# Weight pieces written to SBUF in runs of 1024 or 768 columns instead of 512 or 384

## The chip, the cores and the metric

The kernel runs on one core of a Trainium2 chip. A core has a matrix engine (PE, with its weight loads shown apart as PEld), a vector engine (DVE), a scalar engine (ACT), a general engine (POOL) and a queue engine (SP), an on-chip memory of 128 partitions (SBUF) that they share, and an accumulator memory (PSUM) that PE writes. Sixteen DMA engines move data between the chip's main memory and SBUF. The metric is the device time of one execution in microseconds; before the change the median of three runs is 322.45 us (322.34 to 323.88).

## The reference

Attention for 8 batches, 12 heads, 448 positions and a head dimension of 64, with one extra term in the softmax's denominator, and then a soft mixture of 8 experts with 4 slots each over the 3584 resulting rows:

```python
scores = scale * np.matmul(q, k.transpose(0, 1, 3, 2))
m = np.max(scores, axis=-1, keepdims=True)
e = np.exp(scores - m)
attn = e / (np.sum(e, axis=-1, keepdims=True) + np.exp(-m) + 1e-09)
x = matmul(attn, v)                       # as rows: 3584 x 768
logits = x @ phi                          # 3584 x 32
d = softmax of logits over the rows       # dispatch
slot_input = d.T @ x                      # 32 x 768, 4 slots for each expert
h = np.maximum(slot_input[e] @ w1[e], 0)  # w1[e]: 768 x 1024
slot_out[e] = h @ w2[e]                   # w2[e]: 1024 x 768
c = softmax of logits over the slots      # combine
return c @ slot_out
```

All inputs are float32. The expert weights w1 and w2 are 8 x 768 x 1024 and 8 x 1024 x 768: 50 MB in main memory, 25 MB once they are bfloat16 in SBUF.

## The kernel before

The attention is cut into U = 24 units, each a pair of batches and a pair of heads, and each unit into TB = 7 steps. A step of the main loop (line 802) issues the score matmuls of one step (stage_S, line 256), the transposed scores and their exponentials ten steps behind (stage_ST, lines 300, 305, 309), and whatever the dictionary `plan` holds for that step: the transposes of q and k of the next unit (stage_T, line 241), the product with v (stage_AV, line 336), the normalised rows (stage_N, line 364, on POOL), the transposes of these rows (line 419) and the router's logits. So the order of the work on every engine is written out by hand; nothing is moved by a scheduler.

The expert weights are loaded in 32 pieces in the background of the attention and used only after it, in two passes: w1 in `experts_hidden` (matmul at line 709) and w2 in `outer` (line 825). Piece i is one half of one expert's matrix, 128 partitions of 3072 bfloat16 columns; pieces 0 to 15 are w1 (three rows of 1024 columns a partition), the others w2 (four rows of 768). Pieces 0 to 23 have a place of their own in the tile `wres`, 24 rooms of 3072 columns; pieces 24 to 31 go into `block` once the attention's buffers there are free. A piece of the first kind is loaded as two DMAs of 64 partitions each (lines 782 to 785), at steps 1 and 3 of each of the middle units, some at other places: 48 DMAs at line 180. The remaining 13 DMAs of line 180 are those into `block`, from about 251 us on.

The function `room(i, n)` gives the place of piece i. In `wres` two neighbouring pieces share two rooms and alternate in turns of n columns:

```python
pair = wres[:, ds(i // 2 * 2, 2), :].rearrange("p a n -> p (a n)")
return pair.rearrange("p (k a n) -> p k a n", a=2, n=n)[:, :, i % 2, :]
```

So a piece's columns lie in SBUF in runs of n, each followed by a run of the other piece. The load (load_w, line 167) asks for a room with n // 2, half a row of the weight matrix, 512 columns for w1 and 384 for w2, and views the source in the same halves. A DMA run is then 512 or 384 columns: 2048 or 1536 bytes of float32 read, 1024 or 768 bytes of bfloat16 written. In `block` a piece lies in one stretch. The users take the dictionary `W[kind, e, j]`, a row of the matrix as two halves, and index the half.

The DMAs that change their type on the way (q, k and the weights, float32 to bfloat16) are issued by POOL and go over queue q0; v, which stays float32, is issued by SP (line 159) over q1, and so are the stores of the result (line 889). In each unit POOL issues in this order: the first weight DMA, the normalising product of line 364, the cast of v to bfloat16 (line 314), the second weight DMA, then two q and two k DMAs (line 136) for two units on, which wait until PE has transposed the unit before out of the same buffer. The DMAs of a queue are taken in the order of their issue.

Of the kernel before, what the change touches and what calls it, by code (L numbers as in the profile page):

```python
# [24 lines left out]
def kernel(  # L25
# [93 lines left out]
    def room(i, n):  # L119

        if i >= WRES:
            return block[:, ds(rooms[i - WRES], HW)].rearrange("p (k n) -> p k n", n=n)

        pair = wres[:, ds(i // 2 * 2, 2), :].rearrange("p a n -> p (a n)")
        return pair.rearrange("p (k a n) -> p k a n", a=2, n=n)[:, :, i % 2, :]
# [35 lines left out]
    W = {}  # L161
# [5 lines left out]
    def load_w(i, j0=0, m=None, p0=0, rows=128):  # L167


        kind, e, half = weights[i]  # L170
        if kind == 1:
            J, n = KC // 2, F
            src = moe_w1[e].rearrange("(p j) f -> p j f", p=128)[:, ds(half * J, J), :]
        else:
            J, n = FK // 2, DD
            src = moe_w2[e, ds(half * 128 * J, 128 * J)].rearrange("(p j) f -> p j f", p=128)
        js = ds(2 * j0, 2 * (m or J))
        t_ = room(i, n // 2)
        src = src.rearrange("p j (h n) -> p (j h) n", h=2)
        gdma(out=t_[ds(p0, rows), js, :], in_=src[ds(p0, rows), js, :])  # L180
        for j in range(j0, j0 + (m or J)):
            W[kind, e, half * J + j] = t_[:, ds(2 * j, 2), :]

    first_loads()

# [246 lines left out]
    def mixture(bp, n, at):  # L432
# [98 lines left out]
        if final:  # L531
            at(n - 28, "end", lambda: logits((0, 1)))
            at(n - 2, "end", lambda: logits((2, 3, 4), close=False))
            at(n, "end", lambda: logits((5,)))
            at(n, "end", lambda: gate_logits(0))
            at(n, "end", lambda: warm(1))
            at(n + 2, "small", slot_max)
            at(n + 3, "small", slot_exp)
            at(n + 3, "small", lambda: last_state["lT"]())
            at(n + 4, "end", slots_T)  # L540
            at(n + 4, "end", lambda: last_state["gl"][0]())
            at(n + 4, "end", lambda: warm(1))
            at(n, "load", lambda: nc.gpsimd.memset(SI, 0.0))
            at(n + 5, "small", slot_sum)
            at(n + 7, "end", slot_in)
            at(n + 7, "end", lambda: [load_w(WRES + i) for i in (6, 7)])
            at(n + 7, "end", lambda: gate_logits(1))
            at(n + 7, "end", lambda: last_state["gl"][1]())
            at(n + 7, "end", experts_in)
            at(n + 7, "end", experts_hidden)  # L550
        else:
            for j in range(0, HP, 2):
                at(n - 7 * (HP - 2 - j), "end", lambda j=j: logits((j, j + 1)))
            at(n + 2, "end", slot_max)
            at(n + 5, "end", slot_exp)
            at(n + 6, "value", slots_T)
            at(n + 7, "small", slot_sum)
            at(n + 8, "value", slot_in)
# [195 lines left out]
    for u in range(U):  # L754
        n = u * TB
# [28 lines left out]
    for i, n in enumerate(halves):  # L784
        at(n, "load", lambda i=i: load_w(i // 2, 0, None, i % 2 * P, P))
# [5 lines left out]
    for n, i, js in ((end - 6, 0, (0, 2)), (end - 5, 0, (2, 2)), (end - 2, 1, ()), (end + 2, 2, ()),  # L791
                     (end + 4, 3, (0, 1)), (end + 7, 3, (1, 2)), (end + 9, 3, (3, 1)), (end + 9, 4, (0, 3)),
                     (end + 12, 4, (3, 1)), (end + 12, 5, (0, 3)), (end + 18, 5, (3, 1))):
        at(n, "load", lambda i=i, js=js: load_w(WRES + i, *js))
# [125 lines left out]
```

## Time and profile before

| | |
|---|---|
| median of three runs | 322.45 us |
| the profiled execution | 324.77 us, of which the span from first to last instruction is 323.0 us |
| PE busy | 278.7 us |
| POOL busy | 227.6 us |
| mean granted PE clock | 0.961 (1.00 up to about 290 us) |
| packets on all DMA queues | 48826, 59.34 MB |
| POOL issues of line 180 into wres | 48, 733 ns each on average |
| weight DMA into wres, issue to landing | median 5.7 us |
| q and k DMA into block, issue to landing | median 6.1 and 6.3 us |

The page of the profile gives each engine's busy time, the DMA queues with their packets, bytes written and the time that their packets took as a share of 16 engines, the chain of work that ended last, and the costliest groups of instructions. In a group a column tells how long the engine stood idle before these instructions and what ended it; "issue" there is time in which the engine waited for nothing that the profile shows. A table of stretches gives for each stretch its length, then for each engine its busy time and the number of instructions, the granted PE clock, the DMA share and the GB/s written. The trace also holds a record of every DMA packet: queue, size written, start and duration.

### The profile page before, as it was taken

To read this page: it belongs to the slowest core of one execution; us is meant where nothing else is said; L and a number is where in the kernel's file an instruction comes from. 1 tells how busy PE (TensorE), PEld (TensorE's weight loads), DVE (VectorE), ACT (ScalarE), POOL (GpSimd) and SP (SyncE) were. 2 spreads that over 40 slices of the span, in tenths; PEclk is the share of its full clock that TensorE was granted. 3 is DMA by queue.
4 is the path that set the end of the run, shared out by engine and by line. 5 is a ranking of instruction groups with operands and counts; after the bars stand their busy time and mean duration, and the time that the engine had idled before them with its cause. 6 is when DMAs were issued, how large, how long until landed. Compare 5 with 4: busy or idle time off the path is not lost.

```text
span 323.0 us, 13361 instructions
## 1 busy us (share of the span) xinstructions
PE 278.7 (86%) x5874; PEld 160.4 (50%) x5874; DVE 256.0 (79%) x342; ACT 212.4 (66%) x337; POOL 227.6 (70%) x334
## 2 busy tenths in 40 slices
PE   1669999979999999998999999999999886996910
PEld 1325555546546666555556566555555444652300
DVE  2988988978899999997899999988998845437720
ACT  3025868767778788785777888777877893237610
POOL 6476798888898888987898799989983854620000
PEclk9999999999999999999999999999999999999555
DMA  7979999999999999999899989999998899947997
GB/s 136 157 89 185 172 155 204 180 183 163 174 187 186 143 154 185 182 185 155 131 168 197 156 131 205 167 186 149 162 193 170 117 184 198 194 100 282 398 400 287
DMA packets 48826, 59.34 MB, mean 184 GB/s; under 512 B 4512, under 2 KB 44192, under 8 KB 48768
## 3 DMA queue, kind: packets, MB, share of 16 engines
q0 software_dynamic: 37568, 36.46, 75.8%
q1 hardware_dynamic: 11200, 22.02, 20.4%
q8 instruction: 46, 0.75, 0.9%
q14 instruction: 12, 0.10, 0.1%
HBM read 83.46 MB, written 11.01 MB: 292 GB/s over the span
## 4 chain that ended last, share of the span: by engine, by line
PE 70%; DVE 11%; issue 5%; DMA 4%; POOL 3%; ACT 2%; SPq 0%; DVEq 0%; ACTq 0%; POOLq 0%
PE av L336 16%; PE ps L256 12%; PE ps L300 11%; PE ps L305 8%; PE ps L241 6%; DVE block L264 4%; PE ps L884 3%; PE ps L419 3%; DMA block<-in_k_dram 3%; DVE m L264 2%; PE ps L260 2%; PE ps L825 2%; ACT block L309 2%; PE ps L709 2%; DMA wres<-in_q_dram 1%
## 5 line engine op out<-in xcount | busy, mean ns | idle before, releaser
L309 ACT ACTIVATE block<-ps 128x896 bf16<-128x896 f32 x168 | 153.9, 918 | 57.4 <-PE ps L305 54.4
L264 DVE TENSOR_REDUCE block<-ps 128x2 bf16<-128x896 f32 x84 | 90.8, 1090 | 13.2 <-PE ps L256 11.5
L264 DVE TENSOR_REDUCE m<-ps 128x2 bf16<-128x896 f32 x84 | 90.8, 1091 | 8.8 <-PE ps L256 7.4
L336 PE MATMUL av<-block 64*128 64x65 bf16 (+1 forms) x2688 | 90.4, 194 | 4.7 <-issue 4.0
L336 PEld LDWEIGHTS <-block 64*128 64x128 bf16 (+1 forms) x2688 | 75.6, 97 | 34.5 <-issue 12.6
L300 PE MATMUL ps<-block,ones 64*64 64x448 bf16 x672 | 70.0, 369 | 3.6 <-POOL block L288 1.3
L305 PE MATMUL ps<-block 64*64 64x448 bf16 x672 | 66.5, 354 | 2.0 <-issue 2.0
L256 PE MATMUL ps<-block 64*128 64x448 bf16 x288 | 54.1, 371 | 3.8 <-DVE m L264 1.3
L256 PEld LDWEIGHTS <-block 64*128 64x128 bf16 x288 | 19.8, 94 | 53.0 <-issue 48.4
L282 POOL TENSOR_TENSOR block<-mt,nmask 128x768 bf16<-128x768 bf16 x24 | 35.2, 1469 | 14.3 <-ACT mt L276 12.6
L136 POOL DMA_DIRECT2D block<-in_q_dram x46 | 27.5, 602 | 19.1 <-PE ps L241 17.6
L364 POOL TENSOR_TENSOR block<-block,rec 128x896 bf16<-128x896 f32 x21 | 35.8, 1706 | 0.5
L180 POOL DMA_DIRECT2D wres<-in_moe_w_dram x48 | 35.1, 733 | 1.4
L300 PEld LDWEIGHTS <-ones 64*64 64x64 bf16 x672 | 24.7, 106 | 8.4 <-issue 3.2
L136 POOL DMA_DIRECT2D block<-in_k_dram x46 | 27.8, 620 | 1.2 <-ACT block L309 1.2
L244 DVE COPY block<-ps 128x896 bf16<-128x896 bf16 x48 | 27.8, 617 | 0.3
L305 PEld LDWEIGHTS <-block 64*64 64x64 bf16 x672 | 24.5, 107 | 2.9 <-issue 2.7
L241 PE MATMUL ps<-ident,block 128*64 128x128 bf16 x644 | 24.5, 229 | 0.7 <-DVE m L264 0.4
L314 POOL CAST block<-block 128x896 bf16<-128x896 f32 x24 | 22.5, 938 | 0.8 <-PE ps L305 0.8
L241 PEld LDWEIGHTS <-block 128*64 128x64 bf16 x644 | 20.4, 115 | 3.8 <-issue 1.7
L347 ACT COPY block<-av 128x780 f32<-128x780 f32 x22 | 17.7, 806 | 1.0 <-PE av L336 0.6
L420 DVE COPY block<-ps 128x896 bf16<-128x896 bf16 (+1 forms) x23 | 14.0, 608 | 5.5 <-PE ps L419 5.3
(161 smaller groups left out, 254.5 us busy)
## 6 DMA issues: line engine op xcount, KB each, us to landing
wres<-in_moe_w_dram POOLq DMA_DIRECT2D x48, 384.0 KB, 5.7
out_dram<-wres SPq DMA_DIRECT2D x28, 384.0 KB, 4.6
block<-in_v_dram SPq DMA_DIRECT2D x46, 224.0 KB, 6.1
block<-in_q_dram POOLq DMA_DIRECT2D x46, 112.0 KB, 6.1
block<-in_k_dram POOLq DMA_DIRECT2D x46, 112.0 KB, 6.3
block<-in_moe_w_dram POOLq DMA_DIRECT2D x4, 768.0 KB, 8.4
block<-in_moe_w_dram POOLq DMA_DIRECT2D x3, 384.0 KB, 5.7
block<-in_moe_w_dram POOLq DMA_DIRECT2D x2, 576.0 KB, 8.0
```

The costliest lines, as they stand in the source:

```text
L136: eng.dma_start(out=t_[ds(b * P, P), :, :], in_=src[bp * 2 + b, ds(hp * 2, 2)].rearrange("h (p t) d -> p h (t d)", t=TB))
L180: gdma(out=t_[ds(p0, rows), js, :], in_=src[ds(p0, rows), js, :])
L241: nc.tensor.transpose(ps[ds(h * D, D), :, ds(t * P, P)], r[:, h, ds(t * D, D)], ident)
L244: nc.vector.tensor_copy(t_, ps)
L256: nc.tensor.matmul(ps[:, h, ds(0, S)], QT[u][hs, b, ds(c * 128, 128)], KT[u][hs, b, :], start=True, stop=True)
L264: nc.vector.tensor_reduce(m[:, :, s], ps[:, :, ds(0, S)], axis=AX.X, op=ALU.max)
L282: nc.gpsimd.tensor_tensor(md[:, :, ds(0, C3 * 128)].rearrange("p b (e n) -> p b e n", n=P), mt.unsqueeze(1).unsqueeze(1).broadcast_to([128 ...
L300: nc.tensor.matmul(ps[ds(b * P, P), h, ds(0, S)], ones[hs, :], MD[u][hs, b, :], start=True, stop=False)
L305: nc.tensor.matmul(ps[ds(b * P, P), h, ds(0, S)], KT[u][hs, b, ds(t * P, P)], QT[u][hs, b, :], start=False, stop=True)
L309: nc.scalar.activation(et, ps[:, :, ds(0, S)], AF.Exp, scale=scale)
L336: nc.tensor.matmul(o, et[bs, h, ds(c * 128, w)], V65[u][bs, h, t, ds(0, 65)], start=(t == 0 and h == 0 and c == 0), stop=(t == TB - 1), sk ...
L364: (nc.gpsimd if u < U - 3 else nc.vector).tensor_tensor(x.rearrange("p s (h d) -> p h s d", h=2), xv[:, :, :, ds(0, D)], rec.unsqueeze(3). ...
```

## The change

The load asks for a room with turns of a whole row of the weight matrix, n = 1024 columns for w1 and 768 for w2, and no longer splits the source's rows. Two neighbouring pieces in `wres` still alternate, in turns twice as long. A DMA run is then 4096 or 3072 bytes read and 2048 or 1536 bytes written. `W` still hands out a row as two halves, so its users are as before, as are the order of all instructions, the number of DMAs, and the loads into `block`, whose runs are contiguous in either form.

```diff
         else:
             J, n = FK // 2, DD
             src = moe_w2[e, ds(half * 128 * J, 128 * J)].rearrange("(p j) f -> p j f", p=128)
-        js = ds(2 * j0, 2 * (m or J))
-        t_ = room(i, n // 2)
-        src = src.rearrange("p j (h n) -> p (j h) n", h=2)
+        js = ds(j0, m or J)
+        t_ = room(i, n)
         gdma(out=t_[ds(p0, rows), js, :], in_=src[ds(p0, rows), js, :])
         for j in range(j0, j0 + (m or J)):
-            W[kind, e, half * J + j] = t_[:, ds(2 * j, 2), :]
+            W[kind, e, half * J + j] = t_[:, j, :].rearrange("p (h n) -> p h n", h=2)
```

## The prediction

> **What bounds the kernel now.** I read the page's busy line and DMA queues first, then the waits of the matmul engine, then a table of stretches between its stalls, then the DMA queues inside two short windows.
>
> ```profile
> PE 278.7 (86%) x5874; PEld 160.4 (50%) x5874; DVE 256.0 (79%) x342; ACT 212.4 (66%) x337; POOL 227.6 (70%) x334
> DMA  7979999999999999999899989999998899947997
> ...
> q0 software_dynamic: 37568, 36.46, 75.8%
> q1 hardware_dynamic: 11200, 22.02, 20.4%
> q8 instruction: 46, 0.75, 0.9%
> ...
> L180 POOL DMA_DIRECT2D wres<-in_moe_w_dram x48 | 35.1, 733 | 1.4
> ```
>
> PE is the bound (the chain that ended last is 70% PE), and the DMA engines have a packet on record nearly all the time. q8 matters more than its 0.9%: 46 packets of 0.75 MB in all are 16 KB each, and 0.75 MB over PE's 5874 + 5874 instructions is 64 bytes for each, so q8 carries PE's own program, 256 instructions (128 matmuls with their weight loads) to a packet.
>
> ```profile
> PE av L336 <- issue: 4.0, 8, 0.8
> PE ps L305 <- issue: 2.0, 2, 1.4
> PE ps L419 <- issue: 1.7, 1, 1.7
> ...
> PE ps L300 <- issue: 0.3, 1, 0.3
> ...
> PE ps L241 <- DMA block<-in_k_dram: 0.2, 1, 0.2
> ```
>
> These are PE's waits (total us, times, longest). Data makes PE wait 0.2 us once, for a k load; "issue", where nothing visible is waited for, takes 8.0 us. The next table cuts the span at some of the issue stalls; the first x is the number of matmuls.
>
> ```profile
> 42.41:53.89 11.48, 10.94 (x255) 6.56 (x256) 10.25 (x13) 8.56 (x12) 10.44 (x14) 1.00 1.06 181
> 53.89:65.49 11.60, 11.00 (x255) 6.44 (x255) 10.25 (x13) 8.96 (x14) 9.73 (x15) 1.00 1.06 180
> 65.49:72.32 6.83, 5.45 (x127) 3.45 (x127) 5.45 (x8) 4.10 (x7) 5.49 (x10) 1.00 1.02 180
> 145.88:152.25 6.37, 5.66 (x127) 3.44 (x127) 5.14 (x7) 3.73 (x5) 5.62 (x8) 1.00 0.88 139
> 152.25:158.45 6.20, 5.67 (x128) 3.17 (x129) 5.22 (x6) 4.84 (x7) 4.63 (x7) 1.00 0.92 153
> ```
>
> Between stalls stand 128 or 256 matmuls (one record may be missing): PE stalls exactly where a block of 256 instructions ends and the next has not come. For the stall that ends at 72.32, the DMA queues from the block boundary at 65.49 on:
>
> ```profile
> q0 software_dynamic: 401, 0.39, 73.3%
> q1 hardware_dynamic: 139, 0.23, 18.3%
> ```
>
> and from 69.6 to 70.7:
>
> ```profile
> q0 software_dynamic: 152, 0.14, 80.9%
> q1 hardware_dynamic: 59, 0.10, 29.5%
> q8 instruction: 1, 0.02, 5.9%
> ```
>
> The 16 KB packet did not start for 4.1 us, took 1.03 us, and PE went on 1.65 us after its end. Over all fetches the packet starts 0.5 to 4.4 us after the previous boundary, and PE stalls where it starts later than about 2.5 us before the next. So what q0 and q1 have queued on the engine that carries the fetch reaches PE's time through these stalls: twelve from 20 to 250 us, 6.8 us (0.75, 0.49, 0.59, 1.38, 0.31, 0.44, 0.70, 0.66, 0.52, 0.32, 0.20, 0.44), and one of 1.7 us in the tail.
>
> **The change part by part.** No instruction moves on any engine. The 48 loads of line 180 keep their place, bytes and rows; 32 of them go from 6 runs of 512 to 3 of 1024 a row, 16 from 8 of 384 to 4 of 768. The 13 loads into "block" already have contiguous runs and stay. Packets written go from 12288 of 1024 bytes and 8192 of 768 to 6144 of 2048 and 4096 of 1536.
>
> Engine time of the packets. Median duration in the trace's packet records: 79 ns for 768 bytes, 98 for 1024, 135 for 1536, 248 for 3072, 474 for 6144, so 2048 should be near 173 on that line. Two of 98 become one of 173, two of 79 one of 135: 23 ns less a pair. But the next packet of an engine starts 19 ns before the recorded end of the last, so the engine itself gains 4 ns a pair: 10240 x 4 / 16 = 2.6 us on each engine over the whole run, 0.05 us a load. It is off PE's path except through k and the fetch. The bound above is 23 ns a pair, 0.28 us a load; I take 4, since the successive starts measure it.
>
> The k load. At 35.4 a k load, behind two weight loads in q0, lands 0.14 us before PE uses it and costs the 0.2 us above. Two earlier loads ahead give back 0.1 of it; with the shorter issues below, 0.2. In the other units k lands 0.9 to 3.8 us early (once 0.14), so nothing more is to be had.
>
> POOL. An issue takes 717 ns for 6 runs a row, 753 for 8, 604 (q) to 622 (k) for 2. So 3 runs should take 635 to 663 and 4 runs 655 to 681: 2.9 to 4.2 us less POOL time in all. POOL then waits for PE's transposes before the q loads (17.6 us, 19 times), which swallows it in nearly every unit; two issues at 21 and 23 us are in the chain: -0.15 us.
>
> v loads. They come on q1 and alternate with q0's packets (a 1024-byte packet beside them lasts 174 ns in place of 98). Sixteen packets of v per engine meet 24 of a weight load now and 12 longer ones later: 12 x 154 + 4 x 69 = 2.1 us of q0 between them in place of 16 x 79 = 1.3, so v lands up to 0.85 us later. The cast of v on POOL comes 0.9 to 3.3 us after the landing in 22 units and 0.15 us after in the last but one, where it holds up the first tail load by at most 0.7 us. PE's chain has no wait on that load now; I take 0, at most +0.7. Behind a late cast on POOL stand the next weight load and the q and k loads.
>
> The fetch. What its wait does with longer packets no row shows. In 19 of the 38 fetches before 250 us the packet starts right behind the small write that closes a q0 transfer: there it waits for the transfers ahead as a whole, and these get 0.05 us shorter each, so with two ahead -0.1 us a stall, -1.1 us over twelve. Some start inside a weight load while more is queued: of the stalled ones those at 51.48, 69.64 and 81.33. There about 25 to 30 q0 packets went first. If that is a count, the weight load now fills 12 fewer places, and 12 packets of q or k (69 ns each) go ahead in their stead: +0.83 us each. Between these ends lies the row by packet size: while 1024-byte packets are loaded (20 to 165 us) PE's issue waits are 5.4 us, while 768-byte packets are (165 to 250) 1.0 us, 0.037 against 0.012 a us, and the mean fetch wait is 2.6 against 2.2 us. Place in the run may be the cause, but it points to more wait with longer packets. I take the count for the three fetches where the trace shows the cut, 3 x 0.83 = 2.5, and nothing for the others. Ends: -6.8 us (every stall gone) and 12 x 0.83 = +10.
>
> [...]
>
> Sum: -0.2 - 0.15 + 0 + 2.5 = +2.1 us. The profiled execution took 324.77 us (span 323.0, 1.8 around it), so 326.9 on its scale; it ran 2.3 us over the median of the three runs, 322.45, and on that scale I forecast 324.5.
>
> **The rivals.** No change to speak of: the fetch waits for bytes, not packets. For it: most fetches start at the end of a transfer, and the tail's two long waits (4.4 and 3.7 us) came with packets of 4608 and 6144 bytes, five times as long, and are no longer than the longest before. Against it: the two sizes' rows. Time: -0.35 - 1.1 = 321.0; with v at +0.7, 321.7. Or it waits for one q0 packet in service, 75 ns longer now: 12 x 0.075 = 0.9, less 0.35, 323.0; the 4.1 us in which 401 q0 packets passed on 16 engines, 25 on each, speak against this.
>
> Faster: the 23 ns a pair are real on the engine that carries the fetch, which is the busiest, and the two loads ahead of a fetch end 0.55 us sooner. Each of the twelve stalls shrinks by up to 0.5 us, 5.3 us together, and with the 0.35 above the time is 316.8; half of it gives 319.6. It decides once a load ends 0.1 us sooner than I take it. Against it: the starts 79 ns apart. [...]
>
> Slower for another reason: v, 0.85 us later, delays the cast and with it the next weight, q and k loads, and k's slack of about 1.3 us goes. It needs v over 1.5 us late in most units; then some 0.3 us in each of 20 units, 328.
>
> Or the runs are not read as one, and packets stay as they are: 322.45. The tail's packets of 3072 and 6144 bytes, unsplit, speak against it.
>
> **How the numbers follow.** Longer fetch waits 0.43 (323.5 to 329), late v 0.05 (325 to 329), fetch by bytes 0.30 and by one packet 0.06 (321 to 324), faster 0.14 (316.8 to 320.8), unsplit runs 0.02. Half a percent, 1.6 us, is about what this kernel's measurement can tell from no change. Slower by more 0.47, within 0.38, faster 0.15. The range 320 to 328.5 leaves out most of the faster case and the far end of the slower ones, some 2 in 10; the likeliest case by itself is 323.5 to 329.
>
> **What would show it.** Right: about half the packets in q0's line, the weight issues near 650 ns, more than 8 us of PE issue waits, still 128 matmuls apart, and fetches that start more than 4.1 us after a boundary. Wrong: issue waits unchanged or smaller with the same boundaries, or PE waiting for k or the cast of v.

## The result, and the profile after

The changed kernel took 324.38 us (median of 22 executions, 321.3 to 327.58) and the kernel before, measured beside it, 323.03 us (median of 22, 320.98 to 325.93). The ratio is 1.0052, with an interval of 1.0026 to 1.0077: slower by half a percent, 1.7 us, about the size that this kernel's measurement can tell from no change. The ratio leaves out the slow executions, those over 1.5% above the fastest of their kernel; the means of all 22 executions differ by 0.9 us (ratio 1.0028, standard error 0.0015), and that is not clear of no change.

Single executions of one kernel lie several us apart, and the profiled one after the change (span 319.5 us) happened to be its shortest, so two profiles are not subtracted here; they are read for counts, durations and the place of waits.

From the page of the changed kernel: busy time, the DMA queues, the weight issues and the cast of v.

```profile
PE 278.3 (87%) x5873; PEld 160.9 (50%) x5874; DVE 256.4 (80%) x342; ACT 212.0 (66%) x337; POOL 225.4 (71%) x334
...
q0 software_dynamic: 27328, 36.46, 72.3%
q1 hardware_dynamic: 11200, 22.02, 20.2%
q8 instruction: 46, 0.75, 0.9%
...
L136 POOL DMA_DIRECT2D block<-in_q_dram x46 | 27.6, 605 | 20.3 <-PE ps L240 20.1
...
L179 POOL DMA_DIRECT2D wres<-in_moe_w_dram x48 | 32.7, 683 | 1.9 <-issue 0.6
...
L313 POOL CAST block<-block 128x896 bf16<-128x896 f32 x24 | 22.5, 939 | 0.3 <-DMA block<-in_v_dram 0.2
```

The edit did what it says: 10240 packets fewer on q0, the same bytes, and a smaller share of packet time. POOL issues in 683 ns in place of 733 and hands the gain back as longer waits for PE's transposes (20.1 us in place of 17.6). Lines stand one lower than before. Loads from issue to landing (median us, last column):

```profile
wres<-in_moe_w_dram POOLq DMA_DIRECT2D x48, 384.0 KB, 5.9
...
block<-in_v_dram SPq DMA_DIRECT2D x46, 224.0 KB, 6.5
block<-in_q_dram POOLq DMA_DIRECT2D x46, 112.0 KB, 6.4
block<-in_k_dram POOLq DMA_DIRECT2D x46, 112.0 KB, 6.5
```

All land later than before (5.7, 6.1, 6.1, 6.3), v most of all. That is this profile and not the longer runs: weights, q and k take 5.5, 5.8 and 5.9 us in e6, which has the same runs and v asked for sooner, and 5.0, 5.8 and 5.8 in e2, whose runs are three or four times as long (both are described below). PE's waits from 22 to 250 us (total, times, longest):

```profile
PE av L335 <- issue: 4.5, 8, 1.4
PE ps L299 <- issue: 0.8, 1, 0.8
PE ps L240 <- DMA block<-in_k_dram: 0.8, 2, 0.6
...
PE ps L240 <- DMA block<-in_q_dram: 0.4, 1, 0.4
```

Waits for data are 1.2 us where they were 0.2; the issue waits are 5.3 us where they were 6.4. Together with the waits for other engines, PE waited 8.7 us in this stretch, and 8.9 before. The chain of waits around the longest k wait:

```profile
73.25 1.31 POOL wres L179 x2
74.55 0.19 POOL block L136
...
75.73 0.58 POOL block L136
76.31 9.69 DMA block<-in_k_dram
86.00 0.14 issue
86.13 0.58 PE ps L240 x14
```

POOL issued two weight loads, two q and two k loads back to back (q0's 158 DMAs and q1's 76 landed in the order of their issue in both profiles); the last landed 9.69 us after its issue, when PE was already waiting. Before the change POOL had to wait for PE's transposes ahead of these q loads (first line; the second is the changed kernel):

```profile
78.02 1.19 POOL L136 DMA_DIRECT2D block<-in_q_dram  x2 [1.22 <-PE ps L241]
74.55 1.20 POOL L136 DMA_DIRECT2D block<-in_q_dram  x2
```

The two weight issues ahead were only 0.06 us shorter (1.31 us in place of 1.37). The larger part is PE's: it had stalled for 0.59 and 1.38 us at 65.49 and 72.32, and the profile after has no stall there, so the transposes were done in time.

### The profile page after: what moved, and what is told of

Read it like the earlier page. It is cut to its first block, busy times and chain, and to the rows that moved or that the text cites. A ratio compares the mean times of both kernels' runs of the same rounds, so it can differ in the third digit from the quotient of the medians.

```text
span 319.5 us, 13361 instructions
## 1 busy us (share of the span) xinstructions
PE 278.3 (87%) x5873; PEld 160.9 (50%) x5874; DVE 256.4 (80%) x342; ACT 212.0 (66%) x337; POOL 225.4 (71%) x334
## 3 DMA queue, kind: packets, MB, share of 16 engines
q0 software_dynamic: 27328, 36.46, 72.3%
## 4 chain that ended last, share of the span: by engine, by line
PE 66%; DVE 10%; DMA 7%; issue 5%; POOL 5%; ACT 4%; SPq 0%; ACTq 0%; DVEq 0%; POOLq 0%
PE av L335 14%; PE ps L255 11%; PE ps L299 10%; PE ps L304 8%; PE ps L240 6%; DMA block<-in_k_dram 5%; PE ps L883 4%; ACT block L308 3%; PE ps L418 3%; DVE block L263 3%; DVE m L263 2%; PE ps L259 2%; PE ps L824 2%; PE ps L708 2%; DMA wres<-in_q_dram 1%
## 5 line engine op out<-in xcount | busy, mean ns | idle before, releaser
L136 POOL DMA_DIRECT2D block<-in_q_dram x46 | 27.6, 605 | 20.3 <-PE ps L240 20.1
L179 POOL DMA_DIRECT2D wres<-in_moe_w_dram x48 | 32.7, 683 | 1.9 <-issue 0.6
```

The lines of the kernel that those rows point to most:

```text
L136: eng.dma_start(out=t_[ds(b * P, P), :, :], in_=src[bp * 2 + b, ds(hp * 2, 2)].rearrange("h (p t) d -> p h (t d)", t=TB))
```

## The experiments

Four theories. C is the prediction's: a fetch of PE's program waits for a count of q0 packets. B: only bytes count, and run length means nothing to the fetch. V: long weight packets take turns from v, whose late casts hold up POOL and what stands behind them. D: the q and k loads come late. Ratios are to the kernel before, measured beside each experiment, with 95% intervals; a figure called "all" is the ratio of the means of all executions.

**Run length, both ways (e1, e2, and e1 again as e11).** The source's rows are split in four, or a room is one stretch of 3072 columns:

```diff
-        js = ds(2 * j0, 2 * (m or J))
-        t_ = room(i, n // 2)
-        src = src.rearrange("p j (h n) -> p (j h) n", h=2)
+        js = ds(4 * j0, 4 * (m or J))            # e1, e11: 256 and 192 columns
+        t_ = room(i, n // 4)
+        src = src.rearrange("p j (h n) -> p (j h) n", h=4)
...
-        pair = wres[:, ds(i // 2 * 2, 2), :].rearrange("p a n -> p (a n)")
-        return pair.rearrange("p (k a n) -> p k a n", a=2, n=n)[:, :, i % 2, :]
+        return wres[:, i, :].rearrange("p (k n) -> p k n", n=n)     # e2, over the kernel before
```

(In e1 the matmuls over `W` view their output and operand as two blocks of the shorter run; their number and size stay.)

> The opposite step to the change: runs of 256 and 192 columns (1024 and 768 bytes read) in turns of the same size, same places otherwise, 40960 weight packets in place of 20480. Theory C (a fetch of PE's program waits for a number of q0 packets, whatever their length): the waits get shorter, mean under 2.2 us where before it is 2.6, PE's issue waits from 8 to 5 us, time -1 to -2 us, ratio 0.994 to 0.997. Theory V (long weight packets hold up v on q1 and with it the q and k loads behind): v lands 0.3 us sooner than before, PE's waits for k go, time -0.3 to -1 us. Theory B (only bytes count, packets cost 4 ns each): 20480 more packets cost 5 us on each engine over the run, 0.1 us a load; time +0.2 to +1 us.

> The step beyond the change: each of the 24 pieces lies in one room without taking turns, so a partition's 3072 columns are one run, 12288 bytes read, 6144 written; four weight packets per engine and load. Theory C: 8 more q0 packets go ahead of a fetch than in the changed kernel, +0.55 us at three to six fetches: 2 to 3 us over the changed kernel, ratio to before about 1.013. Theory V: v meets 4 packets of 455 ns and 12 of q and k, 2.6 us of q0 in between in place of 2.1 (changed) and 1.3 (before): about +0.5 us on v's landing against the changed kernel, ratio to before 1.007 to 1.012, more PE waits for q and k and casts waiting for v, fetch waits as they are. Theory B: as the changed kernel or a little faster, and that near before: 0.998 to 1.002.

> e1 once more: runs of 256 and 192 columns, v at its old place. In e1 most executions were 1 to 2 us under before and two far above. Theory V: v gets more of the turns' bytes and comes earlier, but before the change hardly a cast waited, so 0.996 to 1.000. Theory C: the count of packets ahead of a fetch is worth half the time, 0.990 to 0.995.

Measured: e1 0.9936 (0.9891 to 0.9981; all 1.0002), e11 1.0031 (0.9994 to 1.0068; all 0.9988), e2 1.0089 (1.0049 to 1.0128; all 1.0105). The two ratios of one kernel exclude each other, and over all executions they agree. Seven of e1's twelve executions took 318.4 to 320.9 us and five 324.1 to 328.4, and the ratio holds the seven alone. So half a percent hangs on which executions are counted (e1 and e11 were also measured on two chips), and that bears on the change's own 1.0052 too. For 256 columns nothing is settled; 3072 columns are slower either way.

**One matrix alone (e3, e4).** The new runs for one kind of piece only:

```diff
+        h = 1 if kind == 1 else 2     # e3; kind == 2 in e4
-        js = ds(2 * j0, 2 * (m or J))
-        t_ = room(i, n // 2)
-        src = src.rearrange("p j (h n) -> p (j h) n", h=2)
+        js = ds(h * j0, h * (m or J))
+        t_ = room(i, n // h)
+        src = src.rearrange("p j (h n) -> p (j h) n", h=h)
```

> The change for w1 alone (1024 columns, 32 loads up to 160 us), w2 at 384. All theories give it two thirds or more of the change's cost, as two thirds of the loads are w1 and the packets are longer: ratio 1.003 to 1.005. If w2's packets cost it, 1.001 or less.

> The change for w2 alone (768 columns, 16 loads from 167 to 242 us), w1 at 512. All theories: a third or less of the change's cost, ratio 1.000 to 1.002. k has 1.0 to 3.3 us to spare in this stretch, as in the one of w1 apart from the first units, so theory V gives it 1.001 at most; theory C 1.002.

Measured: w1 alone 1.0004 (0.9953 to 1.0055; all 1.0028), w2 alone 0.9975 (0.9924 to 1.0025; all 1.0056). Inconclusive: the halves do not add up to the whole, but their intervals are as wide as the effect.

**v, or q, k and v, out of the way (e5 to e8, e10, e12).** Rooms 22 and 23 of `wres` are empty until step 148. They give v, and in e7 and e8 also q and k, a second place:

```diff
+        t_ = wres[:, WRES - 2, ds(0, 2 * N2)] if u in range(1, 20, 2) else \
+            block[:, ds(parts["vr" if u < U - 1 else "qr"][0], 2 * N2)]
...
-            at(n + (9 if u < U - 2 else 5), "load", lambda u=u: load_v(u + 1))
+            at(n + (6 if u < 19 else 9 if u < U - 2 else 5), "load", lambda u=u: load_v(u + 1))
...
+            if u in range(2, 21, 2):           # e7, e8: q and k too
+                t_ = wres[:, WRES - 1, ds(0, N2)] if name == "qr" else wres[:, WRES - 2, ds(2 * N2, N2)]
```

> v of the odd units 1 to 19 gets a second place in a room of wres that is still empty, and every v up to unit 19 is asked for three steps (about 4.8 us) sooner; weight runs as before the change (512 and 384 columns). All theories: v lands 6 us or more ahead of its cast in place of 2.0, and with these runs little hangs on it, because before the change only one cast waited for v: ratio to before 0.997 to 1.002.

> The same v, with the runs of the change (1024 and 768 columns). Theory V (the longer weight packets take turns from v, whose late casts hold up POOL and what stands behind them): nothing is left to hold up, so 0.998 to 1.001 of e5, 321.5 to 323 us. Theory C of the prediction (a fetch of PE's program waits for a count of q0 packets) and theory D (the q and k loads, not v, come late behind longer runs): the loss stays, 1.004 to 1.007 of e5, 323.5 to 325 us.

> As e5, and q and k of the even units 2 to 20 also get a second place in the empty rooms, so that their loads no longer wait for the transposes of the unit before: POOL's 17 to 26 us of waits for PE at these loads go, and q and k land several us sooner. Runs as before the change. PE's waits for data before were 0.2 us, so theories V and C expect 0.996 to 1.001 of before; if the traffic that is brought forward collides with the fetches, up to 1.005.

> The same places for q, k and v, with the runs of the change. Theory V and theory D: no load is awaited any more, so 0.998 to 1.002 of e7. Theory C: the fetches still wait behind q0 packets, 1.004 to 1.007 of e7.

> v early as in e5, with weight pieces written whole (runs of 3072 columns). e2 with the same runs and v at its old place was 1.009 of before. Theory V: 0.998 to 1.002 of before. Theory C: still 1.007 to 1.010.

> v early as in e5, with runs of 256 and 192 columns. Theory V: the run length no longer matters, 0.998 to 1.002 of before, like e5. Theory C: faster as in e1, 0.990 to 0.995. If both gains add up it is the fastest of all.

Measured:

| runs, columns | v at its old place | v early | q, k, v early |
|---|---|---|---|
| 256 | 0.9936, 1.0031 (all 1.0002, 0.9988) | 0.9975 (0.9941 to 1.0009; all 0.9938) | |
| 512 | 1 | 1.0003 (0.9969 to 1.0037; all 0.9999) | 0.9987 (0.9933 to 1.0040; all 1.0034) |
| 1024 | 1.0052 (1.0026 to 1.0077; all 1.0028) | 0.9971 (0.9924 to 1.0018; all 1.0013) | 1.0020 (0.9983 to 1.0056; all 1.0024) |
| 3072 | 1.0089 (1.0049 to 1.0128; all 1.0105) | 1.0130 (1.0063 to 1.0198; all 1.0073) | |

With v some 12 us ahead of its cast, 1024 columns stand at 0.997 of 512, and with q and k early too at 1.003 of 512, each to about 0.006 (the two intervals added in squares). V expected about 1.000 for both, D for the second alone, and C 1.004 to 1.007 for both. The first pair speaks for V, the second for none of them; over all executions the pairs stand at 1.001 and 0.999. The times do not separate the theories at 1024 columns. At 3072 columns V falls: v is early and the kernel stays 1.3% slower (0.7% over all), about what C expected there, though C's count is excluded below. Its waits of PE, 22 to 250 us, and of POOL over the whole span:

```profile
PE av L337 <- issue: 3.9, 5, 1.4
PE ps L306 <- issue: 2.6, 3, 1.7
PE ps L301 <- POOL block L289: 1.2, 1, 1.2
...
PE ps L420 <- POOL block L365: 0.4, 1, 0.4
```

```profile
POOL block L135 <- PE av L273: 3.1, 1, 3.1
```

POOL stood still ahead of a q load from 212.9 to 215.9 us. The transposes that free the load's buffer had ended at 213.1; the matmul that the row names does not read it. What POOL computed later made PE wait 1.2 and 0.4 us. e2, with the same runs and v at its old place, has the same pause at the same POOL instruction (3.15 us) and the same two waits (1.3 and 0.4). So in both profiles 1.6 us of PE's waiting stands behind that pause; it recurs below. No version was shown to be faster than the kernel before: the best, 256 columns with v early, has an interval that reaches past 1. Over all executions it is 0.9938 (0.991 to 0.997 by two standard errors), so this stays open.

**A dose of late v (e9).** Weight runs as before; v is loaded in half rows, with four DMAs a unit in place of two, so that it lands later:

```diff
+        for b in range(2):
+            for x in range(2):
+                cs = ts(x, N2 // 4)
+                nc.sync.dma_start(out=t_[ds(b * P, P), :, cs],
+                                  in_=v[bp * 2 + b, ds(hp * 2, 2)].rearrange("h (p t) d -> p h (t d)", t=TB)[:, :, cs])
```

> Weight runs, issue order and rooms as before the change; only v of the units from 1 on is loaded in half rows (896 bytes a packet in place of 1792, four DMAs in place of two), so v needs 32 turns beside q0's packets where it needed 16. Theory V (v that lands late is what costs): v lands some 16 turns of 80 to 98 ns later, 1.3 to 1.6 us, twice the delay of the change, and the time is 1.005 to 1.012 of before, with casts that wait for v and waits of PE for POOL or for q and k. Theory C: q0's packets are the same, 0.998 to 1.002.

Measured: 1.0115 (1.0054 to 1.0177; all 1.0078). From its page the group of v's casts (the last column tells what POOL waited for ahead of them), and then two of POOL's waits:

```profile
L323 POOL CAST block<-block 128x896 bf16<-128x896 f32 x24 | 22.4, 933 | 16.9 <-DMA block<-in_v_dram 12.5
```

```profile
POOL block L323 <- DMA block<-in_v_dram: 12.5, 10, 2.4
POOL block L136 <- PE ps L250: 10.3, 7, 4.3
```

From the first issue of a unit's v to its last landing it took 9.23 us, against 7.38 before and 7.79 after the change (means over units 1 to 21). Most of that is SP's: the last of its four issues starts 2.25 us after the first (0.65 with two), and lands 6.98 us later (6.74 before). So e9 prices a late v, and says little of turns on the engines. The median time between landing and cast was 0.15 us, against 2.03 and 1.43. So v that is late enough does cost, and POOL's waits for PE (17.6 us before) absorb a large part of it: 12.5 us of POOL's waiting became 3.7 us.

**What the fetch waits for.** In all profiles the stalls of PE's issue stand at the boundaries of 128 matmuls (127, 128 or 255 apart in the prediction's table). The packet records give what q0 carried between a boundary and the start of the next fetch, per DMA engine, for the fetches that waited over 3.4 us; beside it the mean wait of the first 38 fetches and the sum of PE's stalls at their boundaries:

```
columns  profiles                q0 packets  kB of q0  mean wait  stalls of each profile, us
256      e1, e11, e12            55          31.9      2.32       6.1 1.4 2.6
512      before, e5, e7, e9      33          30.7      2.51       6.4 4.8 5.0 5.3
1024     after, e6, e8           21          30.3      2.54       5.5 5.6 7.9
3072     e2, e10                 12          26.5      2.56       6.6 7.5
```

A fixed count is excluded: at 3072 columns a long fetch wait has 12 packets ahead of it, at 256 columns 55, and with packets twice and six times as long the mean wait is 2.54 and 2.56 us against 2.51 at 512 columns. That the bytes stay near 30 kB shows less than it seems to. The fetches are picked by their wait, and q0 carries about the same in a microsecond at every size (6.8 to 8.4 kB per engine in these waits), so the bytes would stay alike whatever the fetch waits for. What ends the wait was not found.

## Why the prediction was right or wrong

Forecast 324.5 us, +2.1; measured 324.38, +0.52% or 1.7 us (0.8 to 2.5). The number came out, on the slower side that had the largest chance, but the term that carried it does not stand, so that is luck. Part of it is the scale: the forecast stood on 322.45 us, and the kernel before took 323.03 beside the changed one, which by its median is 1.35 us slower and by the means of all executions 0.9.

- **Packets.** Right: 27328 on q0, half of the weights' share; 2048 bytes took 173 ns and 1536 took 135, as forecast. The longer packets brought nothing on the path.
- **POOL's issue.** The direction was right, the size not: 683 ns for 3 runs a row and 682 for 4, against 635 to 663 and 655 to 681. That is 2.4 us of POOL time in place of 2.9 to 4.2. The cover held: the wait for the transposes grew by 2.5 us.
- **The k load** (-0.2). The wait at 35.4 us went, but two others came at k and one at q, 1.2 us together. What the step missed is that PE, with fewer stalls, can reach these loads before they land. That is not the mark of longer runs: such waits add up to 2.4 and 3.7 us at 256 columns (e1, e11) and to 1.9 in e5 at 512, and to nothing in e6, e8, e2 and e10 at 1024 and 3072.
- **v** (0, at most +0.7). The lateness was sized at up to 0.85 us and measured 0.41 on average, in one profile each; with 3072 columns (e2) it is 0.17 (7.55 us), so it does not grow with the runs. The turns themselves are in the starts: beside the usual distance of 79 ns between two packets of 1024 bytes stands one of 161 where v is on record (before), and beside the 154 of 2048 bytes one of 236 (after), 82 more each. The 1024-byte packet itself still lasts 98 ns there by its median, not 174. Two casts waited, 0.11 and 0.16 us; the cast of the last unit but one did not. So the trace shows nearly the 0 that I took. The rival's price was tested by e9: v over 1.5 us late in most units should give about 1.7% (328 on 322.45), and 1.85 us gave 1.15% (0.5 to 1.8). That a late v costs was right, its size somewhat high, and the change's dose is far below it.
- **The fetch** (+2.5, the term that made the number). This is the step that failed. "If that is a count, the weight load now fills 12 fewer places, and 12 packets of q or k (69 ns each) go ahead in their stead": in the table above it is no count. The mean wait went from 2.51 to 2.54 us over the profiles of each size, and the signs named for it did not appear: the issue waits of the changed kernel are 5.3 us, not over 8, and one fetch alone (4.67 us) waited longer than 4.1. The signs named for being wrong did: fewer issue waits at the same boundaries, and PE waiting for k. The stalls at the boundaries average 5.4 us at 512 columns and 6.3 at 1024, with a scatter of 0.7 to 1.4 between profiles: +1.0, not told from 0. The two sizes' rows that made me choose longer waits were place in the run, as the text allowed: in e4 the w1 stretch has packets of 1024 bytes and the w2 stretch longer ones of 1536, and the mean wait is still 2.61 us in the first and 2.29 in the second.
- **What stands in its place is not settled.** The profiles hold no cost to explain: PE's waits from 22 to 250 us add up to 8.9, 8.6 and 9.7 us at 512 columns (before, e5, e7) and to 8.7, 7.7 and 9.5 at 1024 (after, e6, e8); at 256 they are 8.1, 7.0 and 6.4 (e1, e11, e12), at 3072 11.2 and 10.8 (e2, e10). With v early the loss was not seen (0.997 to 512's, give or take 0.006), but the trace of the change shows only 0.3 us of casts waiting, so that v is the cause is not shown. And since half a percent hangs on which executions are counted, a true effect of 0 to 0.5% fits all the runs. The rival of fetches by bytes (-0.35 - 1.1) had no longer waits, as measured, but its gain did not come, and that bytes decide was not shown.

## What to carry to other kernels

A packet's size changed how long a transfer takes by a few nanoseconds a packet (two of 1024 bytes 158 ns from start to start, before; one of 2048 bytes 154, after), and it can delay a load that shares the engines: the first half of a unit's v landed 4.8, 5.0, 6.1 and 6.1 us after its issue with runs of 256, 512, 1024 and 3072 columns (e1, before, after, e2), though the second half hardly followed. Before joining runs in a background load, look at the slack of every load that shares the engines, and at what waits behind its user on the same engine. Where executions scatter by 2% and the effect is half a percent, test a mechanism by a dose several times larger (e9) and by quantities counted in the trace, compare the same kernel in two sessions, and see whether the ratio holds when every execution is counted. A number that comes out right says nothing for the term behind it until that term has been counted.

## What the runs showed of the hardware

**Long stalls of PE were paid twice.** Stretches of e1, the kernel with 256 columns (us, then busy time and instructions of PE, PEld, DVE, ACT and POOL, the granted clock, DMA share, GB/s):

```profile
50.90:54.30 3.40, 1.99 (x48) 1.12 (x42) 2.80 (x3) 1.99 (x3) 3.32 (x4) 1.00 1.29 191
54.70:58.10 3.40, 3.40 (x51) 2.14 (x45) 1.72 (x2) 1.99 (x3) 0.50 (x1) 0.50 1.20 174
58.10:61.50 3.40, 3.40 (x88) 2.13 (x88) 2.68 (x4) 2.15 (x4) 2.62 (x5) 1.00 1.26 221
```

After a wait, the clock stood at one half for 3.4 us, with 51 matmuls where the next stretch has 88. By the trace's clock records the last long stretch at 1.00 lasts 269.65 us before (to 297.9) and 266.24 us after (to 291.7), 79 and 78 times 3.413 us. Over the 14 profiles, cut from 26 to 287 us into windows of 3.41 us on the grid on which the clock changes, the five windows with the least PE time (1.15 to 1.76 us) were each followed by one at half clock; of those between 1.8 and 2.1 us, one in eight was. The clock also halves once between 275 and 280 us in five profiles, with PE busy throughout. The half clock would be a source of the scatter: one stall more or less in the wrong window moves an execution by some 1.4 us, an estimate from the 37 matmuls that the slow stretch fell short by, at 3.4 us for 88. It is not the whole of it: over 247 executions, each taken against the mean of its kernel and session, the time goes with the mean granted clock only in part (correlation -0.43).

**POOL paused ahead of a DMA issue**, at the same instruction for the same runs: 1.34 and 1.32 us (512 columns: before, e5; there between two q DMAs with nothing to wait for), 0.62 to 0.63 (1024: after, e3, e6, e8), 3.15 and 3.06 (3072), 0.76 to 0.77 (256); e9 has 0.91, and e7 none over 0.5. By the kernel's shapes POOL had then asked for about 29,060, 14,720, 14,210 and 41,340 runs on q0. An earlier pause of 1.21 to 1.42 us, between two k DMAs at 110 to 113 us (before, e4, e5, e9), comes at 15,230 runs, and e4 has one of 1.42 us at 28,800; the rows put these down to ACT, whose work had ended 0.87 us before in three of the five. All lie within 6% of one, two or three times 14,400; what makes POOL stop there was not found.
